# Cosine products right behind the sine products on VectorE, each step's two Abs first, and late kernel copies behind them

## The chip, the cores and the metric

The kernel runs on one core of one Trainium2 chip. A core has five engines that each work through a queue of their own in order: TensorE (PE in the profile, its weight loads as PEld), VectorE (DVE), ScalarE (ACT), GpSimd (POOL) and SyncE (SP), which here issues most of the DMAs. Engines wait for one another through semaphores. The metric is the device time of the program in microseconds (us), lower is better. The kernel before took 711.79 us, the median of three runs (710.27 to 713.73).

## The reference

The reference is one block of a network on a sequence of 2048 tokens with 448 channels, all in float32. Its parts, cut to what matters here:

```python
mod = (_silu(c) @ w_mod).reshape(c.shape[0], 6, 1, -1)
sa, ca, ga, sb, cb, gb = (mod[:, 0], ..., mod[:, 5])
h = _layernorm(x, axis=-1) * (1 + ca) + sa
x = x + ga * _A_ref(h, ...)          # a long convolution (S4D)
h = _layernorm(x, axis=-1) * (1 + cb) + sb
x = x + gb * _B_ref(h, ...)          # an MLP over the token axis

# inside _A_ref: the convolution's kernel, per channel d and position l
A = -jnp.exp(log_A_real) + 1j * A_imag
C = (C_real + 1j * C_imag) * dt[:, None]
P = jnp.exp((A * dt[:, None])[:, :, None] * pos[None, None, :])
K = 2.0 * jnp.einsum("dn,dnl->dl", C, P).real
y = jnp.fft.irfft(Uf * Kf[None, :, :], L2)[:, :, :L]     # Uf, Kf: rfft of u and K
```

For each of 448 channels the kernel K is a sum over 256 states of complex exponentials at 2048 positions. That sum is the work which the change touches.

## The kernel before, in words

**How K is built.** A position is written as 64 n + j, so that exp of a multiple of the position is a product of two short factors: G, which depends on n (32 values), and E, which depends on j (64 values). K is then a small matrix product of G and E for each channel. The program takes 16 channels and 128 states at a time. That is one *step*; there are 56 of them (`NHALF`), two for each group of 16 channels. A step of s with even number opens a PSUM tile `kg` and the odd one closes it.

**What a step does.** For step s,

- PE computes the phases of step s + 1 into two PSUM tiles `xe` and `xg` (`st_phase`, matmuls at L609). There are two buffers of each, so the phases of step s + 1 can only be written when step s - 1 has finished reading its own.
- ACT takes the absolute values (`ab` from `xe` at L650, `gs` from `xg` at L651), then four sines: `xe` in place (L652, the sine for E), `gs` (L653, the sine for G), `gs` (L654, the cosine for G) and `xg` from `ab` (L655, the cosine for E, which is written over the phases).
- POOL multiplies the two halves of G with magnitudes (L657, L658).
- DVE multiplies the four quarters of E: two with the sine (L659, L660, the *sine products*), then two with the cosine (L662, L663, the *cosine products*).
- PE multiplies E and G of an earlier step (`st_kgen`, L684, 64 small matmuls): of step s - 2 below step 32, of step s - 1 above it. Behind every odd one ACT copies `kg` to SBUF (`ks`, L698), and DVE adds the skip term to it (L703).

**Other work in the same queues.** The steps also carry the forward transform of u and the inverse transform. Steps 2 to 7 compute LayerNorm statistics on DVE (L500) and modulation vectors on PE (`pm`, L487). Steps 8 to 15 do `u_rows`: matmuls `pu` at L531 and a product on DVE at L534. Steps 16 to 31 do `u_cols`: matmuls at L563, results taken by DVE (L570) or ACT (L572) in turn. Steps 8 to 31 also carry the elementwise preparation of the next parameters, a generator called `chain` that is advanced by `more(n)`. From step 32 on there are *pieces* of the frequency product: matmuls `kx` (L778), two products on DVE (`zx`, `zy`, L787), two sums on POOL (`z`, L789, L790), the inverse matmuls `vv` (L804) and copies on ACT (L810). `st_s1` transforms a finished part of K (`y`, L722; `yk`, L728). Each eighth step is preceded by a *window* of exponentials for eight steps (`mag`, L620).

**What sets the order.** PE, ACT, DVE and POOL have their order written out by hand: each engine executes in the order in which the program emits. Work that waits for a result is put into one of two lists, `dve` and `act`, and emitted when the list is flushed. `act` is flushed at the end of a step, behind its sines. `dve` is flushed by `between()`, which `st_step` calls between the sine products and the cosine products; `between()` also does the statistics and advances `chain`. What a `dve` entry emits need not be for DVE alone: the entry of a piece (`pc_mul`) emits `zx`, `zy` and then the two `z` on POOL, behind the G products of the step because those are emitted ahead of `between()`.

**After the steps** the program finishes the pieces of the second half of the channels, exchanges the result through DRAM, and then runs the MLP: LayerNorm, 672 + 672 matmuls for the two products, with weights split in two parts of reduced precision.

Of the kernel before, what the change touches and what calls it, by code (L numbers as in the profile page):

```python
# [222 lines left out]
def tile_adaln_s4d_mixer(ctx, tc, i, out):  # L223
# [20 lines left out]
    with ExitStack() as es:  # L244
# [117 lines left out]

        dve, act = [], []

# [268 lines left out]
        def st_mag2(s):  # L633
# [5 lines left out]
            m2s[s] = m2  # L639

        def st_step(s, between):
# [5 lines left out]
            xe, xg = phs.pop(s)  # L647
            ab, sg, cg_ = (wp.tile([P, 512], F32, tag=nm, name=nm, bufs=b) for nm, b in (("ab", 1), ("gs", 3), ("gs", 3)))

            S.activation(ab, xe, AF.Abs)  # L650
            S.activation(cg_, xg, AF.Abs)  # L651
            S.activation(xe, xe, AF.Sin, scale=TWO_PI)  # L652
# [7 lines left out]
            V.scalar_tensor_tensor(E[:, 1, :, 31::-1], me[:, :, 31::-1], -1.0, se, ALU.mult, ALU.mult)  # L660
            between()
            V.tensor_tensor(E[:, 0, :, 31::-1], me[:, :, 31::-1], ce, ALU.mult)  # L662
            V.tensor_tensor(E[:, 0, :, 32:64], m2, ce, ALU.mult)  # L663
            eg[s] = (E, Gt)
            mags.pop(s)
# [9 lines left out]
        def st_kgen(s):  # L675
# [16 lines left out]
            if h == 1:  # L692
                p, o = divmod(g, 2)
                if o == 0:
                    kss[p] = wp.tile([P, 2, 4, NJ], F32, tag="ks", name="ks")

                def copy():
                    S.copy(kss[p][:, o], kgs.pop(g))  # L698
                    dve.append(skip)

                def skip():
                    k0 = kss[p][:, o, :, 0:1]
                    tt(k0, k0, dsk[:, g, :, None], ALU.add)  # L703
                    if o:
                        fresh.append(p)

                act.append(copy)

# [269 lines left out]
        def window(s):  # L978
# [9 lines left out]
            for e in range(BATCH):  # L988
# [9 lines left out]
                flush(dve)  # L998
                flush(act)
                if s < 32:  # L1000
                    more(WPACE[s // 8][e])
# [38 lines left out]
        for s in range(tail):  # L1040
# [32 lines left out]

            mellow()
            if s >= NHALF:
                flush(dve)
                mellow()
            else:
                if s < 32 and s % BATCH > 1:
                    st_kgen(s - 2)  # L1080
# [56 lines left out]
        flush(dve)  # L1137
        flush(act)
        assert pieces == [NP, NP] and not kss and next(rest, 0) == next(rows, 0) == next(cols, 0) == 0, pieces
        kgen.close()  # L1140
# [279 lines left out]
```

## Time and profile before

| what | value |
|---|---|
| median of 3 runs | 711.79 us |
| time of the profiled execution | 714.78 us |
| its span in the profile | 712.6 us |
| mean granted TensorE clock | 0.942 |
| PE busy | 630.5 us (88%) |
| DVE busy | 453.8 us (64%) |
| ACT busy | 439.0 us (62%) |
| POOL busy | 272.0 us (38%) |
| stretch of the 56 steps with their windows | about 28 to 370 us |
| rest of the convolution | about 370 to 431 us |
| MLP, close to continuous on PE | 431 to 712.6 us |

A row of the timeline gives start and duration in us, engine, line, operation, the tile written and the tiles read, shapes and, in brackets, for how long the engine sat idle before it and what ended that. Rows of the same kind that follow one another are merged (x4). A row of stretches gives, for each stretch, its length and then busy time and instructions of PE, PEld, DVE, ACT and POOL, the granted clock of TensorE as a share of full speed, the DMA share, and GB/s.

### The profile page before, as it was taken

The numbers are of one execution on the slowest core, as the hardware profiler recorded it, in microseconds if no ns is written. First come the engines' busy times: TensorE is split into PE (matmuls) and PEld (weight loads), VectorE is DVE, ScalarE is ACT, GpSimd is POOL, SyncE is SP. The second block draws the span as 40 slices with busy tenths as digits, with TensorE's granted clock in tenths as the row PEclk, the third lists the DMA queues.
The fourth block names the chain that finished last, engine by engine and source line by source line (L and its number), as shares of the span: only waits on it lengthen the run. The fifth ranks groups of instructions, "written<-read, shape, count | busy, mean of one in ns | idle before, by whom it ended". The sixth has DMA issues, their size and how long they took to land. (4 is left out here: it accounts for less than half of the span.)

```text
span 712.6 us, 18344 instructions
## 1 busy us (share of the span) xinstructions
PE 630.5 (88%) x7228; PEld 458.3 (64%) x7228; DVE 453.8 (64%) x877; ACT 439.0 (62%) x876; POOL 272.0 (38%) x326
## 2 busy tenths in 40 slices
PE   0759879999988889789788979999999999999997
PEld 0434334544535556456455647778999999999996
DVE  7579799679769768576774649777632263344441
ACT  5848697778978889989973559878522242222220
POOL 6487467429629878878774600000000000000000
PEclk9969987789999989899999989999999999999999
DMA  7795555349997635435237979993675536555540
GB/s 172 212 188 140 194 163 187 114 154 242 252 255 242 191 80 129 150 96 157 70 104 227 288 203 254 254 222 99 189 231 137 159 107 174 160 155 155 163 136 26
DMA packets 102259, 121.66 MB, mean 171 GB/s; under 512 B 13114, under 2 KB 87918, under 8 KB 102046
## 3 DMA queue, kind: packets, MB, share of 16 engines
q1 hardware_dynamic: 100638, 113.63, 56.1%
q0 software_dynamic: 1536, 6.87, 4.3%
q8 instruction: 57, 0.93, 0.5%
q14 instruction: 28, 0.23, 0.1%
HBM read 85.11 MB, written 34.87 MB: 168 GB/s over the span
## 5 line engine op out<-in xcount | busy, mean ns | idle before, releaser
L208 ACT CAST whi<-w 128x896 fp32r<-128x896 f32 x64 | 59.7, 938 | 133.4 <-PE o L1387 84.6
L657 POOL TENSOR_TENSOR G<-mag,gs 128x512 f32<-128x512 f32 x56 | 71.9, 1284 | 93.1 <-ACT gs L653 93.1
L217 DVE TENSOR_TENSOR wlo<-w,whi 128x896 fp32r<-128x896 f32 x64 | 68.0, 1086 | 40.3 <-ACT whi L208 27.9
L609 PE MATMUL xg<-tab,lph 64*128 64x512 f32 x112 | 68.5, 613 | 23.8 <-ACT xg L655 7.7
L1317 PE MATMUL acc<-h3h,whi 128*128 128x448 f32 x224 | 82.8, 370 | 0.9 <-ACT h3h L1231 0.9
L1318 PE MATMUL acc<-h3l,whi 128*128 128x448 f32 x224 | 80.9, 361 | 0.7 <-DVE h3l L1238 0.5
L1386 PE MATMUL o<-uh,whi 128*128 128x448 f32 x224 | 81.3, 363 | 0.0
L1319 PE MATMUL acc<-h3h,wlo 128*128 128x448 f32 x224 | 81.3, 363 | 0.0
L1388 PE MATMUL o<-uh,wlo 128*128 128x448 f32 x224 | 81.2, 362 | 0.0
L1387 PE MATMUL o<-ul,whi 128*128 128x448 f32 x224 | 80.6, 360 | 0.0
L684 PEld LDWEIGHTS kg<-E,G 128*32 128x32 f32 x3584 | 60.7, 121 | 30.7 <-issue 16.8
L609 PE MATMUL xe<-tab,lph 64*128 64x512 f32 x112 | 67.2, 603 | 10.2 <-ACT gs L654 6.7
L658 POOL TENSOR_TENSOR G<-mag,gs 128x512 f32<-128x512 f32 x56 | 71.6, 1278 | 0.0
L684 PE MATMUL kg<-E,G 128*32 128x64 f32 x3584 | 70.8, 237 | 0.8 <-issue 0.4
L659 DVE TENSOR_TENSOR E<-m,xe 128x512 f32<-128x512 f32 x56 | 38.3, 683 | 41.1 <-ACT xe L652 33.5
L638 POOL TENSOR_TENSOR m<-mag,w 128x512 f32<-128x512 f32 x56 | 60.3, 1076 | 6.0 <-DVE E L663 1.5
L1390 DVE SCALAR_TENSOR_TENSOR y<-o,b,mod 128x448 f32<-128x448 f32 x16 | 11.0, 685 | 80.2 <-PE o L1388 80.2
L650 ACT ACTIVATE ab<-xe 128x512 f32<-128x512 f32 x56 | 33.7, 601 | 31.9 <-PE xe L609 21.9
L1317 PEld LDWEIGHTS acc<-h3h,whi 128*128 128x128 f32 x224 | 42.1, 188 | 13.1 <-ACT h L1236 4.9
L609 PE MATMUL xe<-tab,lex 64*128 64x512 f32 x56 | 30.1, 547 | 18.2 <-DMA lex<-wm 16.4
L609 PEld LDWEIGHTS xg<-tab,lph 64*128 64x128 f32 x112 | 24.1, 215 | 34.1 <-issue 9.8
L1318 PEld LDWEIGHTS acc<-h3l,whi 128*128 128x128 f32 x224 | 41.9, 187 | 4.0 <-DVE h3l L1238 0.8
(235 smaller groups left out, 1476.3 us busy)
## 6 DMA issues: line engine op xcount, KB each, us to landing
w<-in_B_w_dram SPq DMA_DIRECT2D x64, 224.0 KB
w<-in_B_w_dram SPq DMA_DIRECT2D x32, 448.0 KB
yu_d<-yt SPq DMA_DIRECT2D x16, 448.0 KB
yi<-yu_d SPq DMA_DIRECT2D x32, 224.0 KB
us_d<-uo SPq DMA_DIRECT2D x16, 448.0 KB
u<-us_d SPq DMA_DIRECT2D x32, 224.0 KB
v_d<-vt SPq DMA_DIRECT2D x32, 224.0 KB
vt<-v_d SPq DMA_DIRECT2D x14, 448.0 KB
```

The costliest lines, as they stand in the source:

```text
L217: eng.tensor_tensor(lo, w, hi.bitcast(F32), ALU.subtract)
L609: T.matmul(out[k], lhs[r], rhs[r], start=start, stop=stop)
L638: G.tensor_tensor(m2, me, w[:, :, None].to_broadcast([P, GD, 32]), ALU.mult)
L657: G.tensor_tensor(Gt[:, 1], mg_, v32(sg), ALU.mult)
L658: G.tensor_tensor(Gt[:, 0], mg_, v32(cg_), ALU.mult)
L684: T.matmul(kgs[g][32 * q : 32 * q + 32, m], Gt[:, c, d], E[:, c, d], start=h == 0 and c == 0 and m == 0, stop=h == 1 and c == 1, skip_grou ...
L1317: nc.tensor.matmul(acc[f], hi[:, fs], h3h[:, r], start=r == 0, stop=False)
L1318: nc.tensor.matmul(acc[f], hi[:, fs], h3l[:, r], start=False, stop=False)
L1319: nc.tensor.matmul(acc[f], lo[:, fs], h3h[:, r], start=False, stop=r == 15)
L1386: nc.tensor.matmul(o, hi[:, ks], uh[kh][:, k], start=kh == 0 and k == 0, stop=False)
L1387: nc.tensor.matmul(o, hi[:, ks], ul[kh][:, k], start=False, stop=False)
L1388: nc.tensor.matmul(o, lo[:, ks], uh[kh][:, k], start=False, stop=kh == 1 and k == 6)
```

## The change

Four things are moved; no arithmetic is added or removed.

1. In `st_step` the call of `between()` goes behind the cosine products, so the four products of E follow one another on DVE. The statistics and `chain` then come behind them.
2. The `dve` list is flushed at the start of each step, ahead of the step's products. What earlier steps have left there comes first, on DVE and on POOL.
3. A step's two Abs become a function of their own, `st_abs`, called at the start of the step.
4. The copies of `kg` from step 32 on go into a list of their own, `late_act`, that is flushed behind the next step's Abs instead of behind this step's sines. The windows and the steps past the last one flush it too.

```diff
+        def st_abs(s):
+            xe, xg = phs.pop(s)
+            ab, sg, cg_ = (wp.tile([P, 512], F32, tag=nm, name=nm, bufs=b) for nm, b in (("ab", 1), ("gs", 3), ("gs", 3)))
+            S.activation(ab, xe, AF.Abs)
+            S.activation(cg_, xg, AF.Abs)
+            args[s] = xe, xg, ab, sg, cg_
+
         def st_step(s, between):
...
-            S.activation(ab, xe, AF.Abs)
-            S.activation(cg_, xg, AF.Abs)
+            xe, xg, ab, sg, cg_ = args.pop(s)
...
             V.scalar_tensor_tensor(E[:, 1, :, 31::-1], me[:, :, 31::-1], -1.0, se, ALU.mult, ALU.mult)
-            between()
             V.tensor_tensor(E[:, 0, :, 31::-1], me[:, :, 31::-1], ce, ALU.mult)
             V.tensor_tensor(E[:, 0, :, 32:64], m2, ce, ALU.mult)
+            between()
...
-                act.append(copy)
+                (act if s < 32 else late_act).append(copy)
...
                 flush(dve)
                 flush(act)
+                flush(late_act)
...
             mellow()
+            flush(dve)
             if s >= NHALF:
+                flush(late_act)
                 flush(dve)
                 mellow()
             else:
+                st_abs(s)
+                flush(late_act)
                 if s < 32 and s % BATCH > 1:
                     st_kgen(s - 2)
```

More of the change, by code (lines that the diff above doesn't have):

```diff
@@ L361, in tile_adaln_s4d_mixer @@
         tmp = {}
-        dve, act = [], []
+        dve, act, late_act = [], [], []
         def flush(todo):
@@ L639, in st_mag2 @@
             m2s[s] = m2
+        args = {}
+        def st_abs(s):
[4 more added lines that the diff above has]
+            args[s] = xe, xg, ab, sg, cg_
         def st_step(s, between):
@@ L644, in st_step @@
             Gt = gp_.tile([P, 2, GD, NI], F32, tag="G", name="G")
[L647 to L651, printed above, removed]
+            xe, xg, ab, sg, cg_ = args.pop(s)
             S.activation(xe, xe, AF.Sin, scale=TWO_PI)
@@ L1138, in tile_adaln_s4d_mixer @@
         flush(act)
+        flush(late_act)
+        flush(dve)
         assert pieces == [NP, NP] and not kss and next(rest, 0) == next(rows, 0) == next(cols, 0) == 0, pieces
```

## The prediction

> **What bounds the kernel now.** I read the page first: the busy shares and the chain of work that ended last.
>
> ```profile
> span 712.6 us, 18344 instructions
> PE 630.5 (88%) x7228; PEld 458.3 (64%) x7228; DVE 453.8 (64%) x877; ACT 439.0 (62%) x876; POOL 272.0 (38%) x326
> ...
> PE 42%; DMA 3%; DVE 1%; ACT 0%; SPq 0%; POOL 0%; issue 0%; DVEq 0%
> ```
>
> PE carries 42% of the span in the chain, nearly all of it in the MLP. The change touches only the 56 steps (28 to 370 us) and the work right behind them, so I read stretches next.
>
> ```profile
> 166.20:187.70 21.50, 21.22 (x458) 12.13 (x447) 20.39 (x36) 19.51 (x40) 18.87 (x19) 1.00 0.94 250
> 208.20:227.50 19.30, 19.16 (x317) 10.27 (x316) 17.97 (x32) 15.85 (x33) 14.53 (x15) 0.96 0.77 234
> 293.10:326.90 33.80, 28.01 (x635) 18.53 (x633) 25.58 (x44) 29.87 (x62) 26.78 (x27) 0.90 0.36 106
> 431.00:712.60 281.60, 276.93 (x1366) 249.16 (x1366) 137.31 (x265) 109.81 (x184) 0.00 (x0) 1.00 0.60 163
> ```
>
> In the MLP PE is busy for 276.93 of 281.60 us. It does not change, and what is won or lost ahead of it moves its start. In two stretches of steps 18 to 28 PE is busy for 21.22 of 21.50 and 19.16 of 19.30 us: PE is the bound there. In steps 40 to 47 ACT is busy for 29.87 of 33.80 us and no engine is full: there the steps run at the speed of a loop of waits. The groups of instructions show what a DVE reorder can touch.
>
> ```profile
> L659 DVE TENSOR_TENSOR E<-m,xe 128x512 f32<-128x512 f32 x56 | 38.3, 683 | 41.1 <-ACT xe L652 33.5 <-issue 5.5 <-POOL w L636 0.8
> L703 DVE TENSOR_TENSOR ks<-ks,dsk 128x4 f32<-128x4 f32 x28 | 12.7, 452 | 8.1 <-ACT ks L698 8.1
> ```
>
> DVE sits idle for 41.1 us ahead of the 56 first sine products, mostly until ACT's sine is there. Idle DVE time is not yet time of the kernel; each stage has to be read by itself.
>
> **The change part by part.** The number of instructions stays. Moved are: per step two cosine products (0.68 us each), two Abs, the list `dve` (with `zx`, `zy` and two POOL sums in every second step from 34 on), `chain`, the statistics, and the `kg` copies from step 32 on. ACT's order below step 32 is unchanged, as nothing stands between the Abs's old and new places in its queue. SP's DMAs keep their order but for the stores behind the products of `u_rows`, which come a little earlier; I cost them at nothing, as their loads come steps later.
>
> *Steps 0 to 7.* Step 2's cosine products stand behind statistics that wait for x.
>
> ```profile
> 44.84 0.63 DVE L500 BATCH_NORM_STATS2 st<-xt 128x6 f32<-128x448 f32 x1 [5.12 <-DMA xt<-in_A_u_dram]
> 50.07 0.68 DVE L663 TENSOR_TENSOR E<-m,xg 128x512 f32<-128x512 f32 x1
> ...
> 50.85 0.76 PE L609 MATMUL xg<-tab,lph 64*128 64x512 f32 x1 [7.61 <-issue]
> 52.85 3.35 PE L487 MATMUL pm<-wm,scb 112*128 112x448 f32 x4
> 58.90 1.77 PE L487 MATMUL pm<-wm,scb 112*128 112x448 f32 x4 [0.50 <-DMA wm<-in_w_mod_dram]
> ...
> 42.80:50.80 8.00, 0.43 (x3) 0.12 (x1) 5.90 (x9) 1.91 (x4) 6.51 (x8) 0.70 0.98 190
> 50.80:56.20 5.40, 5.35 (x15) 2.19 (x19) 5.33 (x12) 3.09 (x6) 2.49 (x3) 0.50 0.99 194
> ```
>
> DVE waits 5.12 us for x until 44.84, and the last cosine product ends at 50.75 (50.07 + 0.68). PE, which needs that buffer for the phases of step 4, stands still for 7.61 us. After the change these products come ahead of the statistics, near 40, and PE runs ahead through step 4's phases. But the DVE queue still holds the statistics ahead of step 3's products, so phases 5 come at about 52 (four products of 0.6 behind 49.5, where those of step 2 stand now). And the matmuls `pm` at 58.90 wait for a DMA of w_mod, issued by POOL, which is not earlier. So PE now has an idle stretch of about 5 us right ahead of 58.90, where before it had 0.50. The rows show what that does: the clock was 0.70 in 42.80 to 50.80 and 0.50 in the 5.40 us behind it, and four `pm` took 3.35 us there against 1.77 at 58.90. Late next is PE itself: from 58.90 to the window it is full, so what a slow clock costs is paid. Ends: -0.5 (the clock stays up and the 0.50 wait goes) and +3.4 (half of a slow stretch of 6.8 us, as measured at 100.6 below). I take +2.1, in the middle between 1.6 (`pm` alone, 3.35 - 1.77) and 2.7 (half of 5.40).
> The Trainium skill's page "TensorE: Matmul & The Clock Gate" (section "What's actually happening") says that the clock halves after an idle window of about 3.4 us and comes back after a busy window of that length. The rows above agree in kind; as an estimate from that page, one to two windows would be slow, which costs 1.7 to 3.4 us, and the time would come out between 706.5 and 708.2 instead of 706.9.
>
> *Steps 8 to 15.*
>
> ```profile
> 97.08 0.62 DVE L534 TENSOR_TENSOR yt<-pu,mod 128x448 f32<-128x448 f32 x1
> 99.75 0.68 DVE L663 TENSOR_TENSOR E<-m,xg 128x512 f32<-128x512 f32 x1
> ...
> 100.53 0.64 PE L609 MATMUL xg<-tab,lph 64*128 64x512 f32 x1 [2.80 <-ACT xg L655]
> ...
> 132.25 0.33 PE L722 MATMUL y<-wc,ks 64*64 64x64 f32 x2 [1.25 <-DVE yt L534]
> ...
> 97.70:100.50 2.80, 0.03 (x1) 0.00 (x0) 2.77 (x5) 2.80 (x7) 2.72 (x4) 1.00 0.35 97
> 100.60:107.40 6.80, 6.80 (x86) 3.94 (x87) 6.77 (x10) 5.34 (x10) 6.64 (x8) 0.51 0.26 93
> ```
>
> Here `yt` and `chain` stand between the products: the sine products end at 97.08, the last cosine product at 100.43. After the change it ends near 98.4, so PE's wait shrinks from 2.80 to about 0.7 us and the slow 6.8 us at 0.51 need not follow. But DVE is busy for 6.77 of these 6.80 us: it becomes the bound and gives only the 0.62 us of a `yt` that moves into the idle time ahead of the sine products (about 0.5). The sine products themselves come later than before, by the two or three `yt` now ahead of them; the cosine products, for which PE waits, do not. At 132.25 `y` waited 1.25 us for buffers that `yt` frees; those `yt` now come first. Together -1.8 (0.5 + 1.25). Ends: -3.4 (2.1 + 1.25) and +0.5 (DVE's gain turned round).
>
> *Steps 16 to 27.* 0: PE is full (first two stretches). Should PE have slack, the sine products would be up to 0.6 us later behind a product `uo` (as long as the `yt` above, 0.62) that waits for PE; ends -0.6 and +0.6.
>
> *Steps 28 to 31.*
>
> ```profile
> 229.03 0.67 DVE L663 TENSOR_TENSOR E<-m,xg 128x512 f32<-128x512 f32 x1
> ...
> 229.80 0.46 PE L609 MATMUL xg<-tab,lph 64*128 64x512 f32 x1 [1.78 <-ACT xg L655]
> ...
> 236.96 1.28 POOL L657 TENSOR_TENSOR G<-mag,gs 128x512 f32<-128x512 f32 x1 [1.04 <-ACT gs L653]
> ```
>
> The cosine product at 229.03 stood behind two steps of `chain`; PE waited 1.78 us for it. That goes, but POOL is next: it has only 1.04 us of idle time left ahead of the last G product. -1.0; ends 0 and -1.8.
>
> *Steps 32 to 47.* First, which wait binds ACT to POOL.
>
> ```profile
> 40.44 0.59 ACT L651 ACTIVATE gs<-xg 128x512 f32<-128x512 f32 x1
> 43.34 0.60 ACT L653 ACTIVATE gs<-xg 128x512 f32<-128x512 f32 x1 [1.81 <-POOL G L657]
> ...
> 42.01 1.29 POOL L657 TENSOR_TENSOR G<-mag,gs 128x512 f32<-128x512 f32 x1
> ```
>
> ACT's Abs into `gs` started at 40.44 while POOL's G product of the step before ran until 43.30; the sine at L653 waited for it, 1.81 us. So each step's sine for G waits for L657 of the step before; the Abs does not. Now step 42:
>
> ```profile
> 302.86 1.76 PE L778 MATMUL kx<-yk,si 128*64 128x224 f32 x8
> ...
> 303.28 1.27 POOL L657 TENSOR_TENSOR G<-mag,gs 128x512 f32<-128x512 f32 x1 [0.61 <-ACT gs L653]
> 305.98 0.67 POOL L789 TENSOR_TENSOR z<-zx,zy 128x224 f32<-128x224 f32 x1 [0.19 <-DVE zy L787]
> ...
> 307.25 0.37 ACT L698 COPY ks<-kg 128x256 f32<-128x256 f32 x1 [3.04 <-PE kg L684]
> 307.52 0.60 ACT L650 ACTIVATE ab<-xe 128x512 f32<-128x512 f32 x1
> 309.00 0.61 ACT L653 ACTIVATE gs<-xg 128x512 f32<-128x512 f32 x1
> 314.84 0.60 ACT L650 ACTIVATE ab<-xe 128x512 f32<-128x512 f32 x1
> ```
>
> `kx` ends at 304.62. The products `zx` and `zy` wait for it, and both `z` for them. Before, the G products had gone ahead (303.28); now DVE's sine products and POOL's G products of the step queue behind `zx`, `zy` and `z`. So `z` stays at 305.98, takes 1.24, and G starts at 307.2 instead of 303.28. Its reader, the next sine for G, starts at 308.5. Before it came at 309.00, as ACT waited 3.04 us for PE until 307.25 with the copy and only then did the two Abs. These are now done during that wait (two thirds of 309.00 - 307.52, up to 0.98 us); POOL leaves about 0.45 of it. In the pairs that follow, the loop is: two cosine products 1.3, skip add 0.45, `zx` and `zy` 1.1, `z` 1.24, G 1.27, three sines 1.6 = 7.0 us. Before, a pair took 7.32 (314.84 - 307.52). PE gets its G products later than before and takes part of that, so I take 0.1 a pair: 0.45 + 2 x 0.1 = 0.65 a batch, -1.3 for two. Ends: -2.0 (0.98 each) and +6.0 (second rival). The copy itself costs nothing: its `kg` buffer is next written in the step behind.
>
> *Steps 48 to 58 and what follows.*
>
> ```profile
> 374.12 1.26 PE L804 MATMUL vv<-z,si 64*128 64x224 f32 x8 [1.18 <-POOL z L789]
> 375.85 1.16 PE L722 MATMUL y<-wc,ks 64*64 64x64 f32 x62 [0.22 <-ACT vt L810]
> 378.18 3.36 PE L778 MATMUL kx<-yk,yk 128*64 128x224 f32 x32 [1.17 <-ACT yk L728]
> ...
> 372.62 0.61 DVE L787 TENSOR_TENSOR zy<-kx,u 128x448 f32<-128x448 f32 x1
> ...
> 372.97 0.59 ACT L810 COPY vt<-vv 128x224 f32<-128x224 f32 x2 [1.46 <-PE vv L804]
> ```
>
> Behind the last step the copy of `kg` is now emitted with its skip add at the start of step 57, so `y` of the last part stands ahead of `vv` on PE. Before, PE waited 1.18 us for `z` with `vv`, and `y` began at 375.85. Now `y` needs the skip add, which stands behind `zy` (until 373.23), and two buffers, one freed by `zy`, one by the copy at 372.97; with 0.4 won in the last batch that is 372.9. Then 1.2 for `y`, 1.1 for its two copies, and `kx` starts at 375.3 instead of 378.18: -2.9. `vv` runs beside the copies. Ends: -1.2 (only the idle 1.17 ahead of `kx` goes) and -2.9. The pieces behind are a chain of PE, DVE, POOL and loads whose buffers are freed by it, so it moves as a whole.
>
> **Sum.** 2.1 - 1.8 + 0 - 1.0 - 1.3 - 2.9 = -4.9 us. Against the profiled execution (714.78 us, span 712.6) that is 709.9; that execution lies 3.0 us above the median shown, so for a median I predict 711.79 - 4.9 = 706.9 us.
>
> **Rivals.**
> 1. *The clock stays up in steps 0 to 7.* For it: the skipped wait of 7.61 us keeps PE busier earlier. Against: the DMA that lands at 58.9. Then -0.5 in place of +2.1: -7.5, 704.3 us.
> 2. *POOL's sums in front make the kernel slower.* If the Abs, too, waits for G (the buffers of `gs` are given out in another order once the Abs comes first), then Abs, copy and a sine (0.5 + 0.3 + 0.5 = 1.3) join the loop: 8.3 instead of 7.3, so +1.0 in each of two pairs a batch and as much again at its first pair. Three batches of +3.0 replace -1.3 and the last batch's 0.4: 2.1 - 1.8 - 1.0 - 2.5 + 9.0 = +5.8, 717.6 us. It decides once ACT idles over 0.5 us a pair for L657. For it: POOL is busy for 26.78 of 33.80 us. Against: the Abs at 40.44.
> 3. *The early gains are taken back in the windows* by PE, which is full in much of steps 16 to 28: without the -1.8 and -1.0, -2.1 is left, 709.7 us, no change that can be told.
> 4. *More slow clock*: DVE is the bound in steps 8 to 15, so PE idles in smaller bits; another slow stretch of 5.40 us costs 2.7: 709.6 us.
>
> **How the numbers follow.** Forecast 0.42, rival 1 0.13, rival 2 0.13, rival 3 0.20, rival 4 0.12. About 0.5% (3.6 us) is what a measurement of this kernel can tell from no change: below 708.2 is faster, above 715.4 slower. Faster: 0.36 of the forecast's 0.42, rival 1, and 0.06 of rivals 3 and 4 = 0.55. Slower: rival 2 and 0.02 of the others = 0.15. Same: 0.30. The range runs from 702 (rival 1 with the far ends of steps 8 to 15) to 714 (rivals 3 and 4 together, 712.4, and part of the way to rival 2). The forecast's own range is 704 to 709.5.
>
> **What would show it.** Right: the idle time of PE ahead of step 4's phases is gone; `pm` at its DMA wait takes over 3 us and the clock there is 0.5; the wait of `y` for `yt` is gone; in steps 34 to 54 both `z` come ahead of G on POOL and the idle time of ACT at the copy shrinks; `y` comes ahead of the last `vv`, and the next `kx` starts some 2 to 3 us sooner behind the last step's sines. Wrong: ACT idle for L657 by more than 0.5 us a pair, or a steady pair above 7.4 us; `kx` as far behind as before; or the windows longer by what the steps lost.

## The result, and the profile after

The change makes the kernel slower. The changed kernel takes 723.48 us (median of six executions, 722.68 to 727.86) against 714.58 for the kernel before beside it; the ratio is 1.0155 with a 95% interval of 1.0112 to 1.0198. A second series, in the experiments below, gives 722.02 us and 1.0207 (1.0147 to 1.0268). The prediction was 706.9 us, with a range of 702 to 714. The profiled execution takes 723.22 us with a span of 721.4, against 714.78 and 712.6 before.

One thing has to be known to read any of these numbers. The kernel before, with one and the same program, takes between 702.5 and 725.8 us over 106 executions beside the experiments (mean 714.1, median 714.6), and the time and the granted clock of TensorE go together: an execution of 705.68 us had a mean clock of 0.955, one of 723.94 us had 0.932, and over all 106 the correlation is -0.84, about 4.3 us for each 0.01 of clock. The ratios with intervals leave out executions more than 1.5% above a kernel's fastest. Below I therefore give means over all executions as well, with their standard errors: 714.1 ± 0.5 for before, 723.3 ± 0.6 for the changed kernel (12 executions), a difference of 9.2 us.

The page of the changed kernel, the lines that answer to those of before:

```profile
span 721.4 us, 18371 instructions
PE 633.2 (88%) x7228; PEld 457.7 (63%) x7228; DVE 452.7 (63%) x877; ACT 439.7 (61%) x876; POOL 271.0 (38%) x326
```

The work is the same to within 3 us on every engine; the span is 8.8 us longer. So it is waiting, or PE at a lower clock. The stretches, at the shifted times (columns as before: window, length, busy time of PE, PEld, DVE, ACT, POOL, granted clock, DMA share, GB/s):

```profile
42.80:50.80 8.00, 2.54 (x67) 1.79 (x65) 5.88 (x9) 5.44 (x11) 7.83 (x10) 0.66 0.97 206
50.80:56.20 5.40, 2.82 (x8) 1.19 (x8) 5.33 (x11) 2.50 (x6) 4.36 (x6) 0.50 1.04 172
...
440.00:721.40 281.40, 276.48 (x1366) 248.71 (x1364) 137.15 (x265) 109.47 (x182) 0.00 (x0) 1.00 0.60 162
```

The MLP is as it was (PE busy for 276.48 of 281.40 us), so all of the loss lies ahead of it. From 42.80 to 50.80 us PE is busy for 2.54 us where before it was for 0.43, but in the 5.40 us behind that for 2.82 where it was full. The first sine product of each step on DVE:

```profile
L663 DVE TENSOR_TENSOR E<-m,xe 128x512 f32<-128x512 f32 x56 | 38.0, 679 | 25.8 <-ACT xe L656 23.2 <-PE pm L487 2.5
```

DVE's idle time ahead of the first sine product fell from 41.1 to 25.8 us, as the edit intends. None of these 15 us reached the end.

**Where the time went.** I compare the start of a step's first Abs in the two traces. It is 7.5 us earlier in step 4 (45.1 against 52.6), 3.8 us later in step 6 (66.7 against 62.9), 9.7 us later in step 8 (102.2 against 92.4), 5.8 us later in step 16, 7.5 us later in step 32; the last step's sines end 7.4 us later, the first matmul of the MLP (`acc`) starts 8.4 us later. Steps 2 to 7 first. In the changed kernel L609 are the phases, L663 to L666 the four products of E, L702 the copy of `kg`, L688 its matmuls:

```profile
38.97 0.68 DVE L666 TENSOR_TENSOR E<-m,xg 128x512 f32<-128x512 f32 x1
40.47 0.49 PE L609 MATMUL xe<-tab,lph 64*128 64x512 f32 x1
...
44.85 0.63 DVE L500 BATCH_NORM_STATS2 st<-xt 128x6 f32<-128x448 f32 x1 [5.21 <-DMA xt<-in_A_u_dram]
```

```profile
60.00 3.36 PE L487 MATMUL pm<-wm,scb 112*128 112x448 f32 x4 [5.98 <-DMA wm<-in_w_mod_dram]
63.29 1.93 PE L688 MATMUL kg<-E,G 128*32 128x64 f32 x64
...
65.29 0.37 ACT L702 COPY ks<-kg 128x256 f32<-128x256 f32 x1 [8.50 <-PE kg L688]
```

The first fence is what the change was to do: the cosine products of step 2 are done at 39.65, PE no longer stands 7.61 us ahead of step 4's phases, and DVE waits for x behind them. The second is the price. PE, now ahead, stands for 5.98 us at `pm`, whose operand w_mod lands no earlier than before (60.0 against 58.9). Behind that wait the granted clock is 0.50 until 66.0 us, and `pm` takes 3.36 us instead of 1.77. `kg` and the phases of step 6 come next in PE's queue. They stood behind the same `pm` in the kernel before, where `kg` was faster:

```profile
60.60 1.10 PE L684 MATMUL kg<-E,G 128*32 128x64 f32 x64
```

So step 6 is 3.8 us later (66.73 against 62.89), and the rows add up to that: `pm` starts 1.1 us later and takes 1.6 more, `kg` 0.8 more, and the phases 0.3 more. ACT's idle time of 8.50 us is not the price. Before, ACT stood idle for 7.35 us ahead of step 4's Abs, where PE waited.

**Window 8** took 25.7 us before (from the Abs of step 7 to that of step 8) and takes 31.6 us now. The experiments show what that is worth.

**Steps 8 to 15.** The waits of PE from 84 to 160 us, first before, then after:

```profile
PE xg L609 <- ACT xg L655: 2.8, 1, 2.8
PE xe L609 <- ACT xa L388: 1.8, 1, 1.8
PE y L722 <- DVE yt L534: 1.5, 2, 1.2
PE pu L531 <- DVE yt L534: 0.9, 2, 0.6
```

```profile
PE xg L609 <- DVE E L666: 1.5, 2, 1.0
PE xe L609 <- ACT gs L658: 1.4, 1, 1.4
PE pu L531 <- DVE yt L534: 1.4, 2, 1.1
...
PE pu L531 <- ACT yk L732: 0.7, 1, 0.7
...
PE y L726 <- DVE yt L534: 0.2, 1, 0.2
```

The two long waits are gone, 2.8 to 1.5 and 1.5 to 0.2 us; in their place stand several short ones. In sum PE waits 8.0 us in this window before and 6.9 after.

**Steps 40 to 47**, one pair of steps in the changed kernel, on ACT, PE and POOL (L782 is `kx`, L791 `zx` and `zy`, L793 and L794 `z`, L661 and L662 the G products):

```profile
316.82 0.60 ACT L646 ACTIVATE ab<-xe 128x512 f32<-128x512 f32 x1
324.21 0.60 ACT L646 ACTIVATE ab<-xe 128x512 f32<-128x512 f32 x1
```

```profile
316.43 1.10 PE L688 MATMUL kg<-E,G 128*32 128x64 f32 x64 [0.60 <-POOL G L662]
317.46 0.98 PE L782 MATMUL kx<-yk,si 128*64 128x224 f32 x8
323.83 1.10 PE L688 MATMUL kg<-E,G 128*32 128x64 f32 x64 [0.26 <-POOL G L662]
```

```profile
320.02 0.66 POOL L793 TENSOR_TENSOR z<-zx,zy 128x224 f32<-128x224 f32 x1 [1.17 <-DVE zy L791]
...
321.27 1.27 POOL L661 TENSOR_TENSOR G<-mag,gs 128x512 f32<-128x512 f32 x1
322.50 1.28 POOL L662 TENSOR_TENSOR G<-mag,gs 128x512 f32<-128x512 f32 x1
```

Both `z` stand ahead of G, as foreseen, and the copy of `kg` no longer waits. But a pair takes 7.39 us (324.21 - 316.82) against 7.32 before: `kg` now waits for G, G for `z`, `z` for `kx`, and `kx` stands behind the `kg` ahead of it.

**Behind the last step**, PE first before, then after:

```profile
388.44 0.65 PE L804 MATMUL vv<-z,yk 64*128 64x224 f32 x4 [2.11 <-POOL z L789]
```

```profile
381.30 1.16 PE L726 MATMUL y<-wc,ks 64*64 64x64 f32 x64 [0.45 <-DVE ks L707]
382.39 1.77 PE L808 MATMUL vv<-z,si 64*128 64x224 f32 x8
384.09 3.36 PE L782 MATMUL kx<-yk,yk 128*64 128x224 f32 x32
...
396.43 0.66 PE L808 MATMUL vv<-z,yk 64*128 64x224 f32 x4 [4.18 <-POOL z L793]
...
398.09 2.83 PE L782 MATMUL kx<-yk,yk 128*64 128x224 f32 x16
```

The product on DVE that each of these waits for `z` goes back to, before and after:

```profile
386.49 0.62 DVE L787 TENSOR_TENSOR zx<-kx,u 128x448 f32<-128x448 f32 x1 [2.83 <-DMA u<-us_d]
```

```profile
394.48 0.62 DVE L791 TENSOR_TENSOR zx<-kx,u 128x448 f32<-128x448 f32 x1 [4.90 <-DMA u<-us_d]
```

The queue of SP at the same place, before and after (start, time until the last of the group is issued), and what its loads of `v_d` wait for (total, times, longest):

```profile
380.07 1.23 SPq L1169 DMA_DIRECT2D vt<-v_d  x2
381.36 0.59 SPq L758 DMA_DIRECT2D yk<-in_SI_dram  x1
382.00 1.85 SPq L747 DMA_DIRECT2D u<-us_d  x4
...
SPq L1169 <- DMA v_d<-vt: 1.2, 1, 1.2
```

```profile
384.78 0.54 SPq L818 DMA_DIRECT2D v_d<-vt  x1
...
388.03 1.23 SPq L1180 DMA_DIRECT2D vt<-v_d  x2
389.31 0.59 SPq L762 DMA_DIRECT2D yk<-in_SI_dram  x1
389.95 1.85 SPq L751 DMA_DIRECT2D u<-us_d  x4
...
SPq L1180 <- DMA v_d<-vt: 2.0, 1, 2.0
```

`y` is ahead of the last `vv`, as foreseen, and `kx` comes 8.7 us behind the last sine instead of 10.2. But the last `vv` is now late, so its store leaves SP at 385.32 (384.78 + 0.54), 10.0 us behind the last sine, where before the last store left at 376.44, 8.5 us behind it. The two loads of `v_d` wait for that store (2.0 us, before 1.2), and the loads of `u` stand behind them on SP. They go out 5.9 us behind the start of `kx` (389.95 - 384.09) instead of 3.8 (382.00 - 378.18). DVE waits 4.90 us for `u` instead of 2.83, PE 4.18 us for `z` instead of 2.11, and PE then takes 2.83 us for a `kx` that takes 1.74 elsewhere.

### The profile page after: what moved, and what is told of

Read it like the earlier page. It is cut to its first block, busy times and chain, and to the rows that moved or that the text cites. A ratio compares the mean times of both kernels' runs of the same rounds, so it can differ in the third digit from the quotient of the medians.

```text
span 721.4 us, 18371 instructions
## 1 busy us (share of the span) xinstructions
PE 633.2 (88%) x7228; PEld 457.7 (63%) x7228; DVE 452.7 (63%) x877; ACT 439.7 (61%) x876; POOL 271.0 (38%) x326
## 5 line engine op out<-in xcount | busy, mean ns | idle before, releaser
L661 POOL TENSOR_TENSOR G<-mag,gs 128x512 f32<-128x512 f32 x56 | 72.0, 1285 | 86.9 <-ACT gs L657 86.8
L688 PEld LDWEIGHTS kg<-E,G 128*32 128x32 f32 x3584 | 62.6, 124 | 37.8 <-issue 14.7
L688 PE MATMUL kg<-E,G 128*32 128x64 f32 x3584 | 72.6, 242 | 8.9 <-POOL G L662 5.5
L609 PE MATMUL xe<-tab,lph 64*128 64x512 f32 x112 | 65.9, 592 | 14.0 <-ACT gs L658 7.8
L609 PE MATMUL xg<-tab,lph 64*128 64x512 f32 x112 | 66.7, 598 | 10.5 <-DVE E L666 7.7
L662 POOL TENSOR_TENSOR G<-mag,gs 128x512 f32<-128x512 f32 x56 | 71.7, 1280 | 0.0
L638 POOL TENSOR_TENSOR m<-mag,w 128x512 f32<-128x512 f32 x56 | 59.7, 1066 | 4.6 <-DMA lex<-pars 0.3
L663 DVE TENSOR_TENSOR E<-m,xe 128x512 f32<-128x512 f32 x56 | 38.0, 679 | 25.8 <-ACT xe L656 23.2
L646 ACT ACTIVATE ab<-xe 128x512 f32<-128x512 f32 x56 | 33.6, 601 | 23.4 <-PE xg L609 13.7
L620 ACT ACTIVATE mag<-xe 128x512 f32<-128x512 f32 x56 | 35.6, 636 | 19.3 <-PE xg L609 14.0
L609 PE MATMUL xe<-tab,lex 64*128 64x512 f32 x56 | 31.1, 564 | 18.2 <-DMA lex<-wm 16.0
```

Source lines behind the costliest of these rows:

```text
L609: T.matmul(out[k], lhs[r], rhs[r], start=start, stop=stop)
L661: G.tensor_tensor(Gt[:, 1], mg_, v32(sg), ALU.mult)
L662: G.tensor_tensor(Gt[:, 0], mg_, v32(cg_), ALU.mult)
L688: T.matmul(kgs[g][32 * q : 32 * q + 32, m], Gt[:, c, d], E[:, c, d], start=h == 0 and c == 0 and m == 0, stop=h == 1 and c == 1, skip_grou ...
```

## Experiments

The table collects what the traces of all kernels show: the start of the first Abs of steps 6 and 8, the time from step 8 to step 32, from step 32 to the end of the last step's sines, and from there to the first `acc`; then the mean of all executions of each kernel, with its standard error. *Order* is which of the three parts (steps 0 to 7, 8 to 31, from 32 on) have the new order (n) or that of before (o).

| kernel | order | Abs 6 | Abs 8 | 8 to 32 | 32 to last sine | to `acc` | mean us |
|---|---|---|---|---|---|---|---|
| before | o o o | 62.9 | 92.4 | 156.9 | 118.6 | 55.1 | 714.1 ± 0.5 |
| changed | n n n | 66.7 | 102.2 | 154.6 | 118.5 | 56.2 | 723.3 ± 0.6 |
| e8_changed_again | n n n | 68.0 | 103.5 | 151.7 | 118.5 | 57.5 | (in the line above) |
| e7_early_only | n o o | 67.4 | 103.0 | 153.5 | 118.6 | 53.4 | 717.0 ± 1.1 |
| e6_middle_only | o n o | 63.3 | 101.0 | 152.2 | 117.2 | 52.6 | 712.7 ± 1.3 |
| e3_old_late | n n o | 66.7 | 102.1 | 154.9 | 117.1 | 54.1 | 720.9 ± 1.4 |
| e1_old_first8 | o n n | 63.8 | 102.9 | 156.7 | 119.4 | 56.9 | 724.9 ± 1.6 |
| e2_old_step7 | n n n, step 7 o | 67.7 | 103.2 | 151.6 | 118.5 | 57.5 | 723.0 ± 1.3 |
| e4_warm_pe | n n n | 63.2 | 94.4 | 154.9 | 118.6 | 57.3 | 721.7 ± 1.0 |
| e9_later_pm | n n n | 59.4 | 95.1 | 154.7 | 118.5 | 56.3 | 716.2 ± 1.1 |
| e10_later_pm_old_late | n n o | 60.5 | 93.3 | 152.1 | 117.2 | 52.5 | 712.9 ± 1.0 |
| e11_before_later_pm | o o o | 62.3 | 92.8 | 149.9 | 118.6 | 54.1 | 714.5 ± 1.2 |
| e12_before_last_copy | o o o, last copy n | 62.6 | 98.1 | 158.3 | 117.4 | 56.8 | 717.6 ± 1.6 |
| e5_last_copy | n n n, last copy o | 67.3 | 106.4 | 155.9 | 118.7 | 54.3 | 722.1 ± 1.7 |
| e13_loads_first | n n n | 67.8 | 107.0 | 157.9 | 118.5 | 52.2 | 721.1 ± 2.1 |
| e14_loads_first_later_pm | n n n | 59.6 | 98.8 | 156.3 | 118.6 | 54.6 | 712.9 ± 1.5 |
| e15_best | n n o, last copy n | 58.1 | 99.9 | 156.7 | 118.2 | 55.0 | 711.0 ± 1.3 |
| e16_loads_first_old_copy | n n o | 59.7 | 94.9 | 155.1 | 117.4 | 51.5 | 712.1 ± 0.8 |

### Which part loses the time

The new order is put back to that of before in some steps only, all edits against the changed kernel.

*e1_old_first8*: the order of before in steps 0 to 7.

```diff
             S.activation(xg, ab, AF.Sin, ...)
...
+            if s < 8: between()
             V.tensor_tensor(E[:, 0, :, 31::-1], ...)
             V.tensor_tensor(E[:, 0, :, 32:64], ...)
-            between()
+            if s >= 8: between()
...
-            flush(dve)
+            if s >= 8: flush(dve)
```

> The changed kernel, but in steps 0 to 7 with the order of before (the list of DVE's other work not emptied at the step's head, the statistics between the sine and the cosine products). Theory A (the loss comes from steps 2 to 7 and window 8: PE runs ahead, idles, and its clock halves twice): Abs of step 8 comes back from 102.2 to about 92.4 us, the 4 us that the new order won in steps 8 to 15 stay, and the time is 2 to 5 us below before (ratio 0.993 to 0.997). Rival B (POOL's sums ahead of G in steps 32 to 55 make the loss): the early steps matter little, and the time stays within 3 us of the changed kernel (ratio 1.011 to 1.016). Rival C (what is won early is given back in the later windows, and what is lost early as well, because PE or a DMA sets the end there): ratio 1.00 whatever step 8 does.

Measured: 725.17 us (four executions), ratio 1.0117 (1.0018 to 1.0215). Steps 6 and 7 came back (63.8), step 8 did not (102.9), although all that stands ahead of it is what it is in the kernel before. Theory A in this form is refuted for step 8. In time the edit gains nothing: the mean is 1.6 ± 1.7 us above the changed kernel, which is what rival B expected (within 3 us). What the two traces show at the start of window 8, and over it, before first:

```profile
75.44 1.67 PE L531 MATMUL pu<-xt,wu 32*64 32x448 f32 x8 [0.95 <-POOL xt L518]
```

```profile
76.31 2.47 PE L531 MATMUL pu<-xt,wu 32*64 32x448 f32 x8 [0.93 <-POOL xt L518]
```

```profile
66.70:92.40 25.70, 23.07 (x342) 10.42 (x344) 21.80 (x54) 18.77 (x38) 10.58 (x13) 1.00 0.57 188
```

```profile
67.60:102.90 35.30, 32.99 (x342) 14.12 (x344) 23.43 (x60) 18.92 (x38) 10.60 (x13) 0.67 0.47 161
```

The same matmuls behind the same wait (0.95 and 0.93 us) run at a clock of 1.00 in one execution and 0.67 in the other, and the stretch takes 25.7 or 35.3 us. In the seventeen other traces it takes 27.1 us or more, in e6 and e12, which have the old order up to there as well, 33.9 and 31.7. So the profiled execution of before had the shortest of all, and its 92.4 us for step 8 is no fair base: from one trace each, the 5.9 us that window 8 is longer (31.6 - 25.7), of the 9.7 at step 8, cannot be put down to the change.

*e2_old_step7*: the order of before in step 7 alone (`if s == 7: between()` ahead of the cosine products).

> The changed kernel, but in step 7 alone the statistics stand ahead of the cosine products again. Theory A1 (window 8 loses its 5.9 us because step 7's statistics come later, so the normalised rows come later, PE idles 2.5 us for them and its clock halves at 79.6 us): the wait of pu for xt falls to about 1 us, the clock in window 8 is 1.00, Abs of step 8 comes at 96 to 98 instead of 102.2, and the time falls by 4 to 6 us (ratio 1.007 to 1.010). Rival A2 (window 8 is late only because of what happened ahead of 66 us, and rows come late because DVE is late there): Abs of step 8 moves by under 1.5 us and the ratio stays at 1.013 to 1.016.

Measured: 722.64 us, ratio 1.0147 (1.0090 to 1.0204). The wait of `pu` for the normalised rows fell to 1.16 us as A1 says, but the clock dropped all the same (slow from 80.8 to 91.1 us) and step 8 came at 103.2. These are the numbers of rival A2: the later statistics of step 7 are not what costs (mean 723.0 ± 1.3, the changed kernel 723.3 ± 0.6). Its reason, what happened ahead of 66 us, does not fit e1, where window 8 is longer still.

*e3_old_late*: the order of before from step 32 on (no `flush(dve)` at a step's head, `between()` between the products, copies in `act`).

> The changed kernel, but from step 32 on with the order of before (DVE's list not emptied at a step's head, the list between the products, copies of kg not held back). Theory A (the loss is early): within 2 us of the changed kernel (ratio 1.012 to 1.018). Rival B (POOL's sums ahead of G cost time in steps 32 to 55, and the tail behind them): 4 us or more below the changed kernel (ratio 1.010 or less).

Measured: 718.70 us, mean 720.9 ± 1.4, ratio 1.0120 (1.0060 to 1.0180): 2.4 ± 1.5 us below the changed kernel. Neither theory is met alone: most of the loss is early, some is late. The table says where: from step 32 to the last sine 117.1 against 118.5 us, and from there to `acc` 54.1 against 56.2.

*e6_middle_only* has the new order in steps 8 to 31 alone, *e7_early_only* in steps 0 to 7 alone (conditions as in e1, on `8 <= s < 32` and on `s < 8`; copies in `act`), *e8_changed_again* is the changed kernel beside them.

> The new order in steps 8 to 31 alone; steps 0 to 7, steps 32 to 55 and what follows as before. Theory (the loss is made in steps 0 to 7 and from step 32 on, and the 2 to 4 us won in steps 8 to 31 are real): 1 to 4 us below before, ratio 0.994 to 0.999. Rival (what is won in steps 8 to 15 only makes up for a late start, PE being the bound of the windows): ratio 1.000, with step 32 at the same time behind step 8 as before (156.9 us). Rival (the new order costs time in the middle as well): ratio above 1.003.

> The new order in steps 0 to 7 alone, everything from step 8 on as before. Theory A (waits for w_mod of 6 to 7 us, with a slow clock from 45 to 66 us): steps 6 and 7 come 3.5 to 5 us later than before, and the time is 3 to 6 us above before (ratio 1.004 to 1.009). Rival (steps 0 to 7 have slack up to window 8, and its late start is chance of the clock in single executions): ratio 0.998 to 1.002.

> The changed kernel itself, unaltered, beside the three others, as their measure: 7 to 10 us above before (ratio 1.010 to 1.014). If the parts add up, its distance from before is that of the early order (3 to 6) plus that of the middle (-1 to -4) plus that of step 32 on and the end (2 to 5).

Measured: the middle alone 711.42 us (mean 1.4 ± 1.4 below before; ratio 1.0050, 1.0005 to 1.0095), the early part alone 716.93 us (mean 2.9 ± 1.3 above; ratio 1.0125, 1.0053 to 1.0198), the changed kernel 722.02 us (ratio 1.0207). Mean and ratio of the middle do not agree in sign, so it can't be told from no change. The early part costs 2.9 ± 1.3 us with the rest as before, and 8.2 ± 1.9 with the new middle (e3 less e6).

The parts do not add up. The early part (2.9), the middle (-1.4) and the last copy (3.5, from e12 below) make 5.0 of the 9.2 us. The order from step 32 on costs 12.2 ± 2.1 us when the middle is new and the early steps are old (e1 less e6, with four executions of e1), but 2.4 ± 1.5 in the changed kernel (e3). So what a part costs depends on the others, and how is not resolved.

### What costs in steps 2 to 7: the clock, or the wait

*e4_warm_pe* keeps PE busy in its two waits, ahead of the first `pm` of step 4 and of the first `pu` of window 8, with matmuls whose sums are overwritten.

```diff
+            if k == 2 and 0 in halves:
+                for _ in range(11):
+                    T.matmul(pmods[k], tab[:, 0, 0:P], tab[:, 1, 0:D], start=True, stop=True)
...
+            if n == 0:
+                for _ in range(7):
+                    T.matmul(pm, tab[:, 0, 0:P], tab[:, 1, 0:D], start=True, stop=True)
```

> The changed kernel with nothing moved, but 11 matmuls of 128x448 that do no useful work ahead of the first pm of step 4, which waits for w_mod, and 7 more ahead of the first pu of window 8, which waits for the normalised rows: they only keep PE busy (their sums are overwritten). Theory A with the clock as its cause: pm behind the wait takes 1.77 us instead of 3.36, the clock is 1.00 in most of 60 to 66 and of 79 to 97 us, Abs of step 8 comes 4 to 9 us sooner than 102.2, and the time falls by 4 to 9 us (ratio 1.003 to 1.010). Rival D (it is the order and the waits themselves, the clock only follows): Abs of step 8 stays within 1.5 us of 102.2, or later by the added work, ratio 1.013 or more.

Measured: the trace does what theory A expects (`pm` 1.77 us, step 6 at 63.2, step 8 at 94.4, this execution 716.7 us). The mean of ten executions does not: 721.7 ± 1.0 us, 1.6 ± 1.2 below the changed kernel instead of 4 to 9; the ratio is 1.0176 (1.0115 to 1.0236), as rival D has it. In this trace `pm` still waits for w_mod until 59.22, and keeping PE busy until then puts step 6 where the old order has it (63.2). But a clock that is kept up there does not bring the time back on average.

*e9_later_pm* takes the wait away instead. The matmuls move behind the phases that queued behind them.

```diff
-            if 1 < s < 8:
-                modulation(s // 2, s % 2)
+            if 1 < s < 4:
+                modulation(1, s % 2)
+            if s in (6, 7):
+                modulation(s - 4, 0, 1)
```

> The changed kernel, but the eight pm that wait for w_mod come two steps later (both halves of one in step 6, of the other in step 7), so that the phases of steps 6 and 7 no longer stand behind that wait on PE. Theory W (steps 6 and 7 are late because PE stands 6 us for w_mod with phases queued behind): Abs of step 6 comes at 59 to 63 us instead of 66.7 to 68.0, and the time is 2 to 5 us below the changed kernel (717 to 720). Rival (the same work only comes later, and window 8 takes it back): step 6 as early, but Abs of step 8 at 101 to 105 as in the changed kernel, and the time within 1.5 us of it.

*e10_later_pm_old_late* is the same with e3's edit, *e11_before_later_pm* the same edit in the kernel before.

> The new order in steps 0 to 31, the pm two steps later, and steps 32 to 55 with what follows as before. If the loss of the changed kernel is the wait for w_mod and the stretch behind the last step, and the 1 to 2 us won in steps 8 to 31 are real, it is 0 to 3 us below before (ratio 0.996 to 1.000). Rival (the early order costs by itself, through the statistics that come later than the products): 3 to 6 us above before (ratio 1.004 to 1.009).

> The kernel before with nothing changed but the pm two steps later. Its wait for w_mod was 0.50 us, so theory W gives -1 to +1 us (ratio 0.999 to 1.001). Rival (the later pm are a gain or a loss of their own, which would colour the two runs beside this one): beyond 2 us on either side.

Measured: e9 715.93 us, mean 716.2 ± 1.1, ratio 1.0051 (1.0009 to 1.0092): 7.1 ± 1.3 us below the changed kernel. The trace of e9 at `pm`:

```profile
62.90 3.27 PE L487 MATMUL pm<-wm,scb 112*128 112x448 f32 x8
...
67.63 3.27 PE L487 MATMUL pm<-wm,scb 112*128 112x448 f32 x8
```

No wait stands behind either line, eight matmuls take 3.27 us where four took 3.36, and step 6 starts at 59.4, step 8 at 95.1. Theory W holds, with more than it expected. But step 6 is then 3.5 us earlier than in the kernel before (62.9), so this edit does more than undo a loss: it lets PE keep what it has run ahead. In the kernel before the same move gives 714.54 (mean), +0.5 ± 1.3, so it is no gain of its own. With the old order from step 32 on as well (e10) the kernel is at 712.59 us, ratio 1.0011 (0.9966 to 1.0055): the new order of steps 0 to 31 without that wait costs nothing that can be measured.

### What costs behind the last step

*e5_last_copy*: only the last copy of `kg` is emitted as before. *e12_before_last_copy*: only that copy is emitted as in the changed kernel, all else as before.

```diff
-                (act if s < 32 else late_act).append(copy)
+                (act if s < 32 or s == NHALF - 1 else late_act).append(copy)
```

> The changed kernel, but the last copy of kg (that of the last step) is emitted where it was before, so that the last vv stands ahead of y on PE and its store ahead of the loads behind it on SP. Theory T (the new order behind the last step loses time: kx comes 1.4 us sooner behind the last sines, but SP's loads of u stand behind a store that now comes late, PE waits 4.18 us for z and its clock halves): from the last sine to the first matmul acc 54 to 55 us as before instead of 56.2, and the time 1.5 to 3 us below the changed kernel run beside it. Rival (the gain at kx is kept to the end and the longer stretch is chance of that execution): from the last sine to acc 56 us or more, and the time 0 to 1.5 us above the changed kernel.

> The kernel before with one part of the change alone: the last copy of kg is emitted at the start of step 57, so that y of the last part stands ahead of the last vv. Theory T: the first kx of the second half of the channels comes 1 to 1.5 us sooner behind the last cosine's sine (10.2 us before), but from that sine to the first matmul acc 56 to 58 us instead of 53 to 55, and the time is 2 to 3 us above before (ratio 1.003 to 1.004). Rival (that stretch was longer for another reason, the new order of steps 48 to 55): 53 to 55 us, and the time the same or 1 us below.

Measured: e5 takes 54.3 us from the last sine to `acc`, e12 56.8. In time e12 is 3.5 ± 1.7 us above before (718.08 us, ratio 1.0058, 0.9998 to 1.0118); e5 (721.20 us, mean 1.2 ± 1.8 below the changed kernel) can't be told from it. The stretch itself is clear: over the traces with the copy at its new place, e13 to e15 left aside, it takes 56.2 to 57.5 us (seven traces), with the copy at its old place, e16 left aside, 52.5 to 55.1 (seven traces). The means are 56.9 and 53.7, 3.2 us apart. In all of the first seven the `kx` right behind PE's wait for `z` takes 2.38 to 3.25 us, in all of the others 1.73 or 1.74. In e12 the same lines stand as in the changed kernel:

```profile
381.99 3.36 PE L786 MATMUL kx<-yk,yk 128*64 128x224 f32 x32
...
394.59 1.12 PE L812 MATMUL vv<-z,yk 64*128 64x224 f32 x4 [4.45 <-POOL z L797]
```

*e13_loads_first* is the changed kernel with two loads moved on SP: a table (`yk`) and the first of the four loads of `u` go ahead of those of `v_d`; the other three stay behind them. *e14_loads_first_later_pm* adds this to e9, *e16_loads_first_old_copy* to e10, and *e15_best* is e16 with the last copy at its new place (and `dve` emptied at the start of the steps past the last).

```diff
-        for r in range(2):
-            ln_first(r)
         pc_keep(NP - 1)
         pc_tables(NP)
         pc_load(NP + 3)
+        for r in range(2):
+            ln_first(r)
```

> The changed kernel, but behind the last step SP issues the table and the load of u ahead of the two loads of v_d, which wait for the last store. Theory S (that order is what makes the stretch behind the last step longer): from the last sine to the first acc 52 to 54 us instead of 56.2 to 57.5, PE's wait for z there under 2.5 us instead of 4.18, and the time 3 to 4 us below the changed kernel (718 to 720). Rival (y ahead of vv costs by itself, through the buffers and the later store): 55.5 us or more, the time within 1.5 us of the changed kernel (721 to 724).

> The changed kernel with the later pm and with SP's loads of u ahead of those of v_d. If the wait for w_mod (6 to 7 us with the late pm alone) and SP's order (3 to 4 us) are the loss: 711 to 714 us, as fast as before or up to 3 us faster (ratio 0.996 to 1.000). Rival (there is a third cause, in steps 32 to 55): 716 us or more.

> The new order in steps 0 to 31 and behind the last step, steps 32 to 55 as before, the pm two steps later, SP's loads of u ahead of those of v_d. By theory S the first kx keeps its 1.5 to 2 us and the stretch to acc is 51 to 53 us: 709 to 713 us, 2 to 5 us below before (ratio 0.993 to 0.997). Rival: no faster than before.

> As the kernel with the later pm and the old steps from 32 on (last copy at its old place), with SP's loads of u ahead of those of v_d. Theory S (the late store is what makes that order cost): with the last copy as before SP's loads come in time, so 0 to 1 us below the same kernel without the move, the stretch to acc 52 to 54 us. Rival (the move is a gain by itself, of the size seen in the changed kernel): 50 to 51 us, 3 us below.

Measured: in e13 the stretch takes 52.2 us, and PE's wait for `z` is 2.18 us instead of 4.18. PE and SP of e13:

```profile
392.09 3.36 PE L782 MATMUL kx<-yk,yk 128*64 128x224 f32 x32
...
402.42 0.65 PE L808 MATMUL vv<-z,yk 64*128 64x224 f32 x4 [2.18 <-POOL z L793]
```

```profile
394.32 0.39 SPq L751 DMA_DIRECT2D u<-us_d  x1
395.86 1.23 SPq L1180 DMA_DIRECT2D vt<-v_d  x2
```

The first load of `u` goes out 2.2 us behind `kx` (394.32 - 392.09) instead of 5.9. In this trace theory S holds for the stretch. In e14 and e15, with the same loads moved, it takes 54.6 and 55.0 us, where 51 to 53 were expected of e15. PE's wait for `z` is as short there (1.91 and 2.25 us), but the `kx` behind it takes 3.25 and 2.97 us, in e13 1.73. And e15 against e16, which has the copy at its old place, is still 3.5 us longer in this stretch (55.0 against 51.5), though not in time (-1.1 ± 1.5). In e15 the late store (383.47) is still ahead of that load (385.06) on SP, and DVE waits 2.98 us for `u`, in e16 0.76. So SP's order is part of the cost; how much of it is the clock behind the remaining wait was not separated.

The times of e13 (720.12 us, mean 2.2 ± 2.2 below the changed kernel) are too scattered to show a gain. Between e9 and e14, 12 executions each, the same move gives -3.3 ± 1.9 us. Where the copy is at its old place it gives -0.8 ± 1.3 (e10 to e16), as theory S has it, and -1.0 us of the stretch (52.5 to 51.5), which is between the two forecasts. e14 is at 711.47 us, ratio 0.9971 (0.9926 to 1.0016). So the new order with the two waits mended is as fast as before, and no faster by more than can be measured. e15 at 710.34 us has the lowest median, its mean 3.1 ± 1.4 below before, but its ratio is 1.0000 (0.9963 to 1.0038): better than the changed kernel for certain, better than before not shown.

## Why the prediction was wrong

It erred by 16.6 us (723.48 against 706.9), in the wrong direction, for these reasons, step by step.

- **Base.** The sum was set against a median of 711.79 from three executions. The mean of 106 is 714.1. That is 2.3 us of the error. The 0.5% that it took as what can be told from no change came from the same three executions; the 106 lie up to 3.3% apart. The profiled execution (714.78) was the better base for the total, but its window 8 was the luckiest seen.
- **Steps 0 to 7: +2.1, right mechanism, wrong size.** PE runs ahead, waits for w_mod (foreseen about 5, measured 5.98 us), and `pm` takes 3.36 us at half clock. The term that was too small is the price of that slow stretch, taken between `pm` alone (1.6) and half of 5.40 (2.7). It left out that `kg` and the next phases run at the low clock too (0.8 and 0.3 us) and that `pm` starts 1.1 us later, 3.8 us in all. Step 6 is 4.2 us later on average (67.4 in seven traces with the new order and `pm` where it was, 63.2 in four with the old order). What this costs at the end of the kernel is not one number: 2.9 ± 1.3 us alone (e7) and nothing that e1 can show in the changed kernel (-1.6 ± 1.7); taking the wait away gains 7.1 ± 1.3 there (e9), with step 6 ahead of where it was before the change. Rival 1, the clock that stays up, did not come about.
- **Steps 8 to 15: -1.8, and 28 to 31: -1.0.** The named waits of steps 8 to 15 went (2.8 to 1.5 and 1.5 to 0.2 us), and others came. In steps 28 to 31 PE's wait for `xg` behind DVE's products is 1.8 us before, in one piece, and 1.8 after, in three. The step that failed is that a wait taken away was counted as time won, without the waits that come next. From step 8 to step 32 the traces take 149.9 to 158.3 us with the old order (four traces, mean 154.7) and 151.6 to 157.9 with the new one (fourteen, mean 154.7). e6 gives -1.4 ± 1.4 in time. Rival 3 (early gains taken back) fits this; that PE in the windows is what takes them back was not shown.
- **Steps 16 to 27: 0.** Nothing in the runs speaks against it.
- **Steps 32 to 55: -1.3 and 0.4 in the last batch.** `z` is ahead of G and ACT's wait at the copy is gone. But the pair takes 7.39 us, not 7.2. The loop I summed left PE out: it goes `kg` (316.43), `kx`, `zx` and `zy`, `z` (320.02), both G (to 323.78) and back to `kg` (323.83), 7.40 us. From step 32 to the last sine the new order takes 118.5 to 119.4 us and the old 117.1 to 118.6, so a loss of under a microsecond stands where 1.7 us of gain were. Rival 2 (POOL's sums in front) was right that POOL comes to bind and wrong in its price: ACT's sine for G waits 0.82 us for POOL in one pair and 0.30 in the next (4.2 us in eight waits from step 32 on, 0.5 each, which is just at the sign that rival 2 set), and no Abs waits for it.
- **Behind the last step: -2.9, measured +3.2 by the traces and +3.5 ± 1.7 by e12 (1.2 ± 1.8 by e5).** This is the largest miss. `y` did pass `vv`, and `kx` did come sooner, by 1.5 us. The step that failed is "The pieces behind are a chain ... so it moves as a whole" and "`vv` runs beside the copies": moving `vv` back moves its store, two loads on SP wait for that store, and the loads behind them feed the chain. PE's wait grows from 2.11 to 4.18 us, and the clock behind it drops. The prediction says that SP's DMAs "keep their order" and costs them at nothing. Their order was kept, but the store ahead of those loads left 1.5 us later behind the last sine. I had not followed the moved `vv` into SP's queue.
- **The chances.** Slower had 0.15, by way of rival 2. The loss was found in two places where the forecast had put a small loss and its largest gain. With both waits mended (e14) the kernel is 1.1 ± 1.6 us below before. That the two account for the loss one by one is not shown, as the parts do not add up.

## What to carry to other kernels

When an engine is let run ahead, look for the next thing in its queue that waits for a DMA: it runs ahead only as far as that. Price what is queued behind the wait too, not only the instruction that waits, because here all of it ran at the low clock. Follow each moved instruction to the transfers that it releases and into the queue of the engine that issues them, because one load that waits for a late store holds up every load behind it. Where the same program scatters by 3%, compare stretches over many traces and means over many executions; one pair of profiles put 5.9 us on window 8, and three traces with the old order ahead of it (e1, e6, e12) are as long there or longer.

## What was not expected of the hardware

The granted clock of TensorE differs between executions of the same instructions with the same waits, as the stretches of before and e1 show (1.00 and 0.67). Over 106 executions time and mean clock go together (correlation -0.84); the correlation alone does not say which of the two drives the other. The clock changes at 32.4, 39.2, 46.1 and 56.3 us in the trace of before, at 31.9, 38.7, 45.5 and 59.2 in that of e1. The distances (6.8, 6.9, 10.2 and 6.8, 6.8, 13.7 us) are two, three or four times 3.41 us. The Trainium skill, "TensorE: Matmul & The Clock Gate", section "What's actually happening", says that the clock is set from a free-running window of 3413 ns that does not start with the kernel; these traces agree, with steps that lie 0.5 us apart in the two. The section also says that the ramp penalty is under 1% of a typical kernel's span. The 3.3% between executions of one program here (702.5 to 725.8 us) is not that penalty alone: in the trace of before the clock drops again at 46.1 us, long behind the start.

The clock can also stay low while PE is busy. In e1:

```profile
89.90:110.40 20.50, 20.50 (x180) 9.61 (x178) 13.90 (x34) 13.54 (x26) 3.85 (x4) 0.50 0.57 201
```

PE is busy for all of 20.50 us at a clock of 0.50, six times 3.41 us. The section's rule that one busy window brings the clock back does not describe this stretch; why the clock stayed low was not tried.
